# Two query tiles of batch 1 transposed by DMA, and the loads of batch 2 moved behind them

## The chip, the cores and the metric

The kernel runs on one core of a Trainium2 chip. The metric is device time in microseconds: 323.51 us, the median of 3 runs (323.31 to 323.75). One execution was also recorded by the profiler. Its own time is 322.91 us, of which 321.1 us lie between its first and its last instruction. All times below that have a place in the execution count from its first instruction.

## The reference

Eight batches go through cosine-weighted linear attention and then through one gated feed-forward layer. Cut to what matters:

```
r = relu(x); phi(x) = concat(r * cos(theta), r * sin(theta))    # theta = pi/2 * pos / 576
kv  = einsum('bhsf,bhsd->bhfd', phi(k), v)       # per head 128 x 64, sum over 576 positions
z   = sum over positions of phi(k)
x   = (phi(q) @ kv) / (phi(q) @ z + 1e-6)        # 8 batches, 8 heads, 576 positions, 64 wide
xn  = x / sqrt(mean(x*x) + 1e-6) * rms_g         # 4608 rows of 512
out = (silu(xn @ w_gate) * (xn @ w_val)) @ w_out # 512 -> 1536 -> 512
```

q, k and v are 8 x 8 x 576 x 64 in float32, and the weights are 512 x 1536, 512 x 1536 and 1536 x 512.

## The kernel before

**Blocks.** The rows of the feed-forward layer are worked off in nine blocks of 512 rows: block b holds 512 rows of batch b, and one further block ("8") holds the 64 rows that are left over of each batch. A block has 16 steps. In steps 0 to 11 the function `gval_step` computes one slice of 128 hidden columns: four matmuls of the gate into bank `psG`, four of the value into `psV` (line 556), then Silu on ACT and a product on DVE into `hT`. In steps 12 to 15 `out_step` multiplies `hT` by `w_out` (line 574), 12 matmuls for each of four tiles of 128 rows, and ACT copies each result out to `osb`, which SP stores. Block 0 has its own forms of the last steps: `last_step` is its step 11, and `out_first` runs its 48 output matmuls, numbered i = 0 to 47, over four banks.

**Side work.** While the matmuls of block b run, the attention of batch b+1 is made in small pieces, and these pieces are hung by hand on (block, step, place) with `at(...)`. "pe" is ahead of the step's matmuls, "mid" between them, "pre" and "post" ahead of and behind the step's Silu and product. In block 0's last steps `at(0, 12, i, ...)` hangs a piece ahead of output matmul i. For one batch nb the pieces are, in order:

- `load_kv` and `load_q`: 1.1 MB each from DRAM into `raw`, a ring of five buffers. SP issues most of them; for batches 1 and 2 GpSimd (POOL) does.
- `k_phi` (line 294 on DVE, line 292 on ACT) and `v_cast` (line 288): phi(k) and v in bf16.
- `q_phi`, the same for q, in four tiles j of 128 rows, and then the transposition of each tile into `qpT`. From batch 2 on it is a DMA transpose that SP issues (`q_tr_dma`, line 346). In batch 1 all four are made by TensorE (`q_tr_pe`, line 363, eight transposes each) with a copy out of PSUM (`q_tr_evac`).
- `kvz_pe`: the sums kv and z on TensorE (line 394, from batch 3 on line 387), copied to `kvzs` by ACT.
- `nd_pe` (line 449): numerator and denominator of tile j into `psA`; `nd_post`: the division on DVE (lines 489, 492, 499).
- `x_sq`: the mean square on ACT (line 515), and the power -1/2 on POOL (line 520); `x_norm` (line 527) on DVE makes `xn`.
- `x_tr_dma` (line 540): a DMA transpose on SP into `xnT`, which the next block multiplies. Tile 3 of batch 1 is transposed by TensorE instead (`x_tr_pe`, line 546), with a copy by DVE.

Each engine, SP and POOL among them, works off its instructions in the order of the program. So a piece that waits holds up all that stands behind it on its engine. `psG`, `psV` and `psC` have two banks each; `psA` is single, so `nd_pe` of a tile waits for `nd_post` of the tile before.

**Around the change.** In block 0, POOL issues k of batch 2 behind step 8 and v of batch 2 behind step 10. They stand in POOL's DMA queue behind the weights `wo`. `last_step` ends with `nd_pe(1, 0)`, the eight transposes of tile 2, and `nd_post(1, 0)`. In `out_first`, tiles 1 to 3 of batch 1 follow at matmuls 6, 11 and 19, each with the norm and the transpose of the tile before; the transposes of q tile 3 stand at matmul 9, `load_q(2)` and the last norm at 21, and `x_tr` of tile 3 at 43.

Of the kernel before, what the change touches and what calls it, by code (L numbers as in the profile page):

```python
# [10 lines left out]
BF16 = mybir.dt.bfloat16  # L11
# [6 lines left out]
def kernel(  # L18
# [17 lines left out]
    HP = H // 2  # L36
# [10 lines left out]
    V, A, G = nc.vector, nc.scalar, nc.gpsimd  # L47

    ctx.enter_context(tc.manual_schedule())
    one = ctx.enter_context(tc.tile_pool(name="one", bufs=1))  # L50
# [8 lines left out]
    psV = [ps.tile([P, 512], FP32, name=f"psV{i}") for i in range(2)]  # L59
# [10 lines left out]
    def kv_rows(src, b, hps):  # L70
        return src[b, 2 * hps[0] : 2 * hps[1], :, :].rearrange(
            "(hp hh) (s c) d -> (hh s) hp (c d)", hh=2, c=NC
        )

    def wide(b):
        return b > 2
# [21 lines left out]
    def raw_kv(which, b):  # L98
        t = raw_tile(which, b)
        if wide(b):  # L100
            return t[:, :].rearrange("p (h e) -> p h e", h=H)
        return t[:, 0 : HP * NC * D].rearrange("p (hp e) -> p hp e", hp=HP)
# [4 lines left out]
    def load_kv(which, b, hps=(0, HP), eng=nc.sync):  # L107
        src = k if which == "k" else v
        if not wide(b):
            return eng.dma_start(  # L110
                out=raw_kv(which, b)[:, hps[0] : hps[1], :], in_=kv_rows(src, b, hps)
            )
        last = KP if b < B - 1 else KP - 1
        for r0, r1 in ((0, KM), (KM, last)):
            eng.dma_start(
                out=raw_kv(which, b)[r0:r1, :, :], in_=kv_rows5(src, b, r0, r1)
            )
        if last < KP:
            eng.dma_start(
                out=raw_kv(which, b)[last:KP, :, :].rearrange("p h (c d) -> p h c d", d=D),  # L120
                in_=src[b, :, S - 1 : S, :].rearrange("h s d -> s h d").unsqueeze(2)
                .to_broadcast([1, H, NC5, D]),
            )
# [25 lines left out]
    for c0, c1 in ((0, 4), (4, NC)):  # L149
        nc.sync.dma_start(  # L150
            out=raw_kv("k", 0)[:, :, c0 * D : c1 * D],
            in_=kv_rows(k, 0, (0, HP))[:, :, c0 * D : c1 * D],
# [70 lines left out]
    for i in range(3):  # L223
        m, e = math.frexp(left)
# [6 lines left out]
    def g_spread(bank, t):  # L231
# [12 lines left out]
        out=th[:, 0:NTAB], in0=fidx[:, :], scalar1=S - 1.0, scalar2=ang,  # L244
        op0=ALU.min, op1=ALU.mult,
    )
    for c0, c1, i0, less in ((0, 9, 0, 576.0), (13, 14, 13, 64.0), (19, NTAB, 13, 64.0)):
        V.tensor_scalar(
            out=th[64:128, c0:c1], in0=fidx[64:128, i0 : i0 + c1 - c0],
# [4 lines left out]
        out=th[:, NTAB : 2 * NTAB], in0=th[:, 0:NTAB], scalar1=math.pi / 2.0,  # L254
# [4 lines left out]
        out=sel[:, :, :], in_=ident[0:4, 0:4].unsqueeze(2).to_broadcast([4, NDT, P])  # L259
# [57 lines left out]
    def q_phi(eng, b, j, part):  # L317
        o = slice(0, D) if part == 0 else slice(D, F)
        f = cos_of if part == 0 else sin_of
        phi(eng, qp_of((b, j))[:, :, o], raw_q(b)[:, :, j * D : (j + 1) * D], f(9 + j))  # L320
# [23 lines left out]
    def q_tr_dma(b, j):  # L344
        t = qp_of((b, j))
        nc.sync.dma_start_transpose(
            out=qpT[:, :, j * P : (j + 1) * P], in_=t[:, :, :].rearrange("p h f -> p (h f)")
        )
# [10 lines left out]
    def q_tr_pe(b, j, bank):  # L359
        t = qp_of((b, j))  # L360
        dst = bank.bitcast(BF16).rearrange("p (h s) -> p h s", h=H)
        for h in range(H):
            nc.tensor.transpose(dst[:, h, :], t[:, h, :], ident[:, :])  # L363

    def q_tr_evac(eng, b, j, bank):
        dst = bank.bitcast(BF16).rearrange("p (h s) -> p h s", h=H)
        copy(eng, qpT[:, :, j * P : (j + 1) * P], dst)
# [111 lines left out]
    x_of, rs_of, xn_of = {}, {}, {}  # L479
# [31 lines left out]
    def x_sq(b, j):  # L511
        xt = x_of[(b, j)]
        scr = one.tile([P, DM + 1], BF16, name="scr", tag="scr")
        ms = four.tile([P, 1], FP32, name="ms", tag="ms")
        A.activation(  # L515
            out=scr[:, :], in_=xt[:, 0 : DM + 1], func=AF.Square,
            scale=1.0 / math.sqrt(DM), accum_out=ms[:, :],
        )
        rs = four.tile([P, 1], FP32, name="rs", tag="rs")
        G.tensor_tensor(out=rs[:, :], in0=ms[:, :], in1=mhalf[:, :], op=ALU.pow)  # L520
        rs_of[(b, j)] = rs
# [231 lines left out]
    def at(blk, n, where, f, *args):  # L753
        slots.setdefault((blk, n), {}).setdefault(where, []).append((f, args))

    def run(blk, n, where):
        for f, args in slots.get((blk, n), {}).get(where, []):
            f(*args)

    KCS = ((0, 1, 2), (3, 4), (5, 6), (7, 8))  # L760
    KCS5 = ((0, 1), (2,), (3,), (4,))
    for c in range(NC):
        at(0, 5 + c // 3, "post", k_phi, V, 1, c, 0)
        at(0, 5 + c // 3, "post", k_phi, A, 1, c, 1)
    for j in range(4):
        at(0, (8, 8, 9, 10)[j], "post", q_phi, V, 1, j, 0)
        at(0, (8, 9, 10, 10)[j], "post", q_phi, A, 1, j, 1)
        bank = (psC[0], psC[1], psV[0], psV[1])[j]
        if j < 2:
            at(0, 10 + j, "pe", q_tr_pe, 1, j, bank)  # L770
            at(0, 10 + j, "pre", q_tr_evac, V, 1, j, bank)
    at(0, 8, "post", load_kv, "k", 2, (0, HP), G)
    at(0, 9, "post", v_cast, G, 1, (0, 2))
    at(0, 10, "pre", v_cast, V, 1, (2, 4))
    at(0, 10, "post", load_kv, "v", 2, (0, HP), G)

    def q_tr(j, bank):
        q_tr_pe(1, j, bank)  # L780
        q_tr_evac(A, 1, j, bank)

    def x_first(j):
        nd_pe(1, j)
# [11 lines left out]
    def last_step():  # L796
        n = NNT - 1
        g, v = banks_of(0, n)
        run(0, n, "pe")
        half_mm(0, n, wg, g)  # L800
        kvz_pe(1)
        sg = four.tile([P, TB], FP32, name="sg", tag="sg")
        A.activation(out=sg[:, :], in_=g[:, 0:TB], func=AF.Silu)
        kvz_evac(A, 1)
        run(0, n, "pre")
        half_mm(0, n, wv, v)
        nd_pe(1, 0)
        q_tr(2, psV[0])
        nd_post(1, 0)
        V.tensor_tensor(out=hT[:, n, :], in0=v[:, 0:TB], in1=sg[:, :], op=ALU.mult)  # L810
        x_sq(1, 0)
        run(0, n, "post")

    for j, i in ((1, 6), (2, 11), (3, 19)):
        at(0, 12, i, x_first, j)
        at(0, 12, i, x_last, j - 1)
    at(0, 12, 9, q_tr, 3, psV[0])
    at(0, 12, 21, x_norm, 1, 3)
    at(0, 12, 21, load_q, 2)
    at(0, 12, 43, x_tr, 3, psV[0])  # L820
    for nb in range(2, B):
        b = nb - 1
        first = nb == 2
        for i, cs in enumerate(KCS5 if wide(nb) else KCS):
            kb, kn = ((0, 14), (0, 15), (1, 0), (1, 1))[i] if first else (b - 1, 12 + i)
            for c in cs:
                at(kb, kn, "post", k_phi, V, nb, c, 0)
                at(kb, kn, "post", k_phi, A, nb, c, 1)
        for i in range(2):
            vb, vn = ((0, 15), (1, 0))[i] if first else (b - 1, 13 + 2 * i)  # L830
            at(vb, vn, "post", v_cast, V, nb, (2 * i, 2 * i + 2))
        for j in range(4):
            late = j + (nb == 3)
            qb, qn = (b, 1 + j) if first else (b - (late < 2), (14 + late) % 16)
            at(qb, qn, "post", q_phi, V, nb, j, 0)
            at(qb, qn, "post", q_phi, A, nb, j, 1)
            at(qb, qn, "post", q_tr_dma, nb, j)
        kz = 3 if first else 2
        at(b, kz, "pe", kvz_pe, nb)
        at(b, kz, "pre", kvz_evac, A, nb)  # L840
        for j in range(4):
            n = ((6, 8, 9, 11) if first else (4, 6, 8, 10))[j]
            at(b, n, "mid" if n == 9 else "pe", nd_pe, nb, j)
            at(b, n, "pre", nd_post, nb, j)
            at(b, n, "post", x_sq, nb, j)
            m = n + 2 if first and j == 0 else n + 1
            at(b, m, "post", x_norm, nb, j)
            at(b, m, "post", x_tr_dma, nb, j)

    for pair in range(4):  # L850
        b = 2 * pair or 3
        at(*((2, 13), (1, 13), (3, 9), (5, 9))[pair], "post", load_q_tails, pair)
        at(b, 3, "post", q_tails_phi, V, pair, 0)
        at(b, 3, "post", q_tails_phi, A, pair, 1)
        at(b, 3, "post", q_tails_tr_dma, pair)
        at(b, 12, "pe", nd_tails_pe, pair)
        at(b, 12, "pre", nd_post, 2 * pair + 1, 4)
        at(b, 12, "post", x_sq, 2 * pair + 1, 4)
        at(b, 13, "post", x_norm, 2 * pair + 1, 4)
        at(b, 13, "post", x_tr_dma, 2 * pair + 1, 4)  # L860
    for nb in range(3, B):
        b = nb - 2
        for which, n in zip("kvq", {1: (4, 8, 12), 2: (3, 5, 8)}.get(b, (0, 3, 6))):
            if which == "q":
                at(b, n, "post", load_q, nb)
            else:
                at(b, n, "post", load_kv, which, nb)
# [91 lines left out]
```

## Time and profile before

| what | value |
|---|---|
| median of 3 runs | 323.51 us |
| profiled execution, its own time | 322.91 us |
| span of its instructions | 321.1 us |
| TensorE matmul busy | 313.6 us, 98% of the span |
| DVE, ACT, POOL busy | 185.4, 165.8, 40.5 us |
| share of TensorE in the chain that ended last | 94% |
| block 0's output matmuls begin | 42.33 us |
| block 1 begins | 54.09 us |
| block 2 begins | 87.51 us |
| granted TensorE clock | 1.00 |

The busy share says how much of the time an engine worked, not what the end waited for. The chain of work that ended last is followed back from the last instruction to what released each step, and so names what set the end. "q0" is the queue of the DMAs that POOL issues, and "q1" that of SP's; both move their data over the same 16 DMA engines, and a share above 100% means that packets overlap. "To landing" is the time from a DMA's issue until its data is there.

### The profile page before, as it was taken

How to read it: one execution, taken by the hardware profiler on the slowest of the kernel's cores; microseconds unless marked ns; L12 is line 12 of the kernel's file. 1: busy time of each engine (PE TensorE's matmuls, PEld its weight loads, DVE VectorE, ACT ScalarE, POOL GpSimd, SP SyncE). 2: the span in 40 equal slices, each digit the busy share in tenths (PEclk: the TensorE clock that was granted, in tenths of full speed). 3: DMA queues.
4: the chain of work that ended last, by engine and by line, in shares of the span. 5: the costliest groups of instructions: out<-in, count | busy, mean ns of one | idle time of the engine just before them, and what ended most of it. 6: DMA issues, size and time to landing. Idle time of an engine off the chain costs nothing.

```text
span 321.1 us, 6023 instructions
## 1 busy us (share of the span) xinstructions
PE 313.6 (98%) x2274; PEld 162.4 (51%) x2310; DVE 185.4 (58%) x382; ACT 165.8 (52%) x322; POOL 40.5 (13%) x79
## 2 busy tenths in 40 slices
PE   7999999999999999999999999999999999999996
PEld 2689564544454445444544445544544444444444
DVE  7976977668457773777457644781676034204410
ACT  5766756754574466554744575446543233223321
POOL 9771211002001100010001100100011000000000
PEclk9999999999999999999999999999999999999999
DMA  7999999788999999999799959995522500041002
GB/s 232 239 270 269 282 329 227 201 183 190 223 226 211 187 263 187 221 247 182 162 186 230 197 163 200 197 217 163 99 59 41 116 33 0 0 102 31 1 35 98
DMA packets 80092, 53.76 MB, mean 167 GB/s; under 512 B 52235, under 2 KB 74047, under 8 KB 80063
## 3 DMA queue, kind: packets, MB, share of 16 engines
q1 hardware_dynamic: 73110, 41.25, 62.1%
q0 software_dynamic: 6944, 12.13, 15.5%
q8 instruction: 18, 0.29, 0.4%
q14 instruction: 12, 0.09, 0.1%
q10 hardware_dynamic: 8, 0.00, 0.0%
HBM read 37.83 MB, written 9.44 MB: 147 GB/s over the span
## 4 chain that ended last, share of the span: by engine, by line
PE 94%; DMA 2%; DVE 1%; issue 1%; POOL 1%; ACT 0%; POOLq 0%; ACTq 0%
PE psC L574 27%; PE psV L556 27%; PE psG L556 26%; PE psV L643 2%; PE psA L449 2%; DMA vv<-in_v_dram 2%; PE psG L574 2%; PE psG L643 2%; PE psA L387 2%; PE psA L394 1%; PE psA L474 0%; PE psV L363 0%; PE psG L430 0%; PE psC L546 0%; POOL raw L135 0%
## 5 line engine op out<-in xcount | busy, mean ns | idle before, releaser
L571 DVE TENSOR_TENSOR hT<-psV,sg 128x512 bf16<-128x512 f32 x99 | 68.2, 689 | 96.5 <-PE psV L556 64.1
L556 PE MATMUL psV<-xnT,wv 128*128 128x512 bf16 x344 | 89.6, 379 | 0.7 <-issue 0.2
L570 ACT ACTIVATE sg<-psG 128x512 f32<-128x512 f32 x99 | 58.6, 592 | 60.8 <-PE psG L556 52.7
L556 PE MATMUL psG<-xnT,wg 128*128 128x512 bf16 x337 | 88.5, 379 | 0.7 <-issue 0.2
L574 PE MATMUL psC<-wo,hT 128*128 128x512 bf16 (+1 forms) x400 | 88.4, 376 | 0.4
L574 PEld LDWEIGHTS <-hT 128*128 128x128 bf16 x456 | 43.1, 98 | 47.7
L556 PEld LDWEIGHTS <-wv 128*128 128x128 bf16 x400 | 39.0, 98 | 46.8
L556 PEld LDWEIGHTS <-wg 128*128 128x128 bf16 x400 | 37.0, 98 | 39.9 <-DVE xnT L288 0.2
L520 POOL TENSOR_TENSOR rs<-ms,mhalf 128x1 f32<-128x1 f32 x36 | 20.5, 570 | 193.9 <-ACT scr L515 193.7
L286 ACT COPY osb<-psC 128x512 f32<-128x512 f32 x32 | 18.7, 585 | 49.9 <-PE psC L574 46.1
L515 ACT ACTIVATE scr<-xt 128x513 bf16<-128x513 f32 x36 | 22.8, 635 | 23.3 <-DVE xt L499 22.3
L527 DVE SCALAR_TENSOR_TENSOR xn<-xt,rs,gb 128x512 bf16<-128x512 f32 (+1 forms) x37 | 26.9, 730 | 9.9 <-POOL rs L520 9.9
L292 ACT ACTIVATE kp<-raw,tab 128x256 bf16<-128x256 f32 (+2 forms) x51 | 28.8, 607 | 2.4 <-DMA raw<-in_k_dram 2.4
L499 DVE TENSOR_TENSOR xt<-psA,rec 128x512 f32<-128x512 f32 x36 | 24.9, 691 | 1.2
L292 ACT ACTIVATE qp<-raw,tab 128x512 bf16<-128x512 f32 (+1 forms) x36 | 23.3, 666 | 1.2 <-DMA raw<-in_q_dram 1.1
L294 DVE TENSOR_SCALAR kp<-raw,tab 128x256 bf16<-128x256 f32 (+2 forms) x53 | 20.1, 428 | 0.5 <-DMA raw<-in_k_dram 0.5
L294 DVE TENSOR_SCALAR qp<-raw,tab 128x512 bf16<-128x512 f32 (+1 forms) x34 | 15.3, 463 | 4.7 <-DMA raw<-in_q_dram 4.7
L449 PEld LDWEIGHTS <-qpT 128*128 128x128 bf16 x224 | 10.6, 97 | 6.6
L556 PE MATMUL psV<-xnT_tail,wv 128*128 128x512 bf16 x48 | 12.3, 379 | 0.1
L556 PE MATMUL psG<-xnT_tail,wg 128*128 128x512 bf16 x46 | 12.0, 379 | 0.1
L288 DVE CAST vv<-raw 116x1280 bf16<-116x1280 f32 (+1 forms) x13 | 11.1, 857 | 1.3 <-DMA raw<-in_v_dram 1.3
L449 PE MATMUL psA<-kvzs,qpT 128*128 128x65 bf16 x224 | 11.4, 193 | 0.0
(102 smaller groups left out, 177.7 us busy)
## 6 DMA issues: line engine op xcount, KB each, us to landing
out_dram<-osb SPq DMA_DIRECT2D x27, 256.0 KB, 2.3
raw<-in_q_dram SPq DMA_DIRECT2D x6, 1024.0 KB, 9.1
raw<-in_k_dram SPq DMA_DIRECT2D x5, 1120.0 KB, 8.8
raw<-in_v_dram SPq DMA_DIRECT2D x5, 1120.0 KB, 9.4
raw<-in_k_dram POOLq DMA_DIRECT2D x2, 1152.0 KB, 19.2
raw<-in_v_dram POOLq DMA_DIRECT2D x2, 1152.0 KB, 15.7
out_dram<-osb SPq DMA_DIRECT2D x17, 128.0 KB, 2.6
wg<-in_moe_w_gate_dram POOLq DMA_DIRECT2D x3, 512.0 KB, 13.8
```

The source lines that it names most:

```text
L286: A.copy(out=o, in_=i)
L292: A.activation(out=out_ap, in_=in_ap, func=AF.Relu, scale=scale)
L294: eng.tensor_scalar(out=out_ap, in0=in_ap, scalar1=scale, scalar2=0.0, op0=ALU.mult, op1=ALU.max)
L449: nc.tensor.matmul(heads[:, g, hp, :], lhsT=qpT[:, h, j * P : (j + 1) * P], rhs=kvzs[b][:, g, hp * E : (hp + 1) * E], start=True, stop=True,)
L499: V.tensor_tensor(out=xt[:, 0:DM].rearrange("p (hp g d) -> p g hp d", g=2, d=D), in0=heads[:, :, :, 0:D], in1=rec[:, :, :].unsqueeze(3).to ...
L515: A.activation(out=scr[:, :], in_=xt[:, 0 : DM + 1], func=AF.Square, scale=1.0 / math.sqrt(DM), accum_out=ms[:, :],)
L520: G.tensor_tensor(out=rs[:, :], in0=ms[:, :], in1=mhalf[:, :], op=ALU.pow)
L527: V.scalar_tensor_tensor(out=xn_of[(b, j)][:, c], in0=x_of[(b, j)][:, c], scalar=rs_of[(b, j)][:, :], in1=gb[:, c], op0=ALU.mult, op1=ALU. ...
L556: nc.tensor.matmul(bank[:, cols[0] : cols[1]], lhsT=w[:, t, n * P : (n + 1) * P], rhs=x[:, t, cols[0] : cols[1]], start=(t == 0), stop=(t ...
L570: A.activation(out=sg[:, :], in_=g[:, 0:TB], func=AF.Silu)
L571: V.tensor_tensor(out=hT[:, n, :], in0=v[:, 0:TB], in1=sg[:, :], op=ALU.mult)
L574: nc.tensor.matmul(bank[:, 0 : cols[1] - cols[0]], lhsT=hT[:, n, j * P : (j + 1) * P], rhs=wo[:, n, cols[0] : cols[1]], start=(n == 0), st ...
```

## The change

- The transposes of q tiles 2 and 3 of batch 1 are no longer made by TensorE and copied by ACT. A new `q_last` makes their cosine half on DVE at the end of `last_step` (it stood behind steps 9 and 10) and issues a DMA transpose on SP for each.
- POOL issues k of batch 2 at the end of `last_step`, behind the power of tile 0, and v of batch 2 in a new `load_held`, behind a copy of one element that waits for the last norm of batch 1.
- In `out_first` tiles 1, 2 and 3 move to matmuls 8, 16 and 24, the last norm and `load_q(2)` to 25, and `x_tr` to 42.
- The side work of batch 2 moves to later steps of block 1: `k_phi` to steps 0 to 3 (it began in block 0), `v_cast` to steps 2 and 3 and from DVE to POOL, `q_phi` and its transposes from steps 1 to 4 to steps 3 to 6, `kvz_pe` from 3 to 5, `nd_pe` from 6, 8, 9 and 11 to 7, 9, 10 and 12, with each norm one step behind.
- Batch 3: `load_q` moves from step 12 of block 1 to step 14, `k_phi` and `v_cast` one step later, `q_phi` one step later (its first is now behind step 0 of block 2), `nd_pe` in block 2 from steps 4, 6, 8, 10 to 5, 7, 9, 11. The load of the left-over q rows of batches 2 and 3 moves from step 13 of block 1 to step 15.
- The one-row loads for the last row of k and v of batch 7 are issued by POOL and no longer by SP.

```diff
@@ load_kv
         if last < KP:
-            eng.dma_start(
+            G.dma_start(
                 out=raw_kv(which, b)[last:KP, :, :].rearrange("p h (c d) -> p h c d", d=D),
...
-    KCS = ((0, 1, 2), (3, 4), (5, 6), (7, 8))
+    KCS2 = ((0, 1), (2, 3), (4, 5), (6, 7, 8))
...
     for j in range(4):
-        at(0, (8, 8, 9, 10)[j], "post", q_phi, V, 1, j, 0)
+        if j < 2:
+            at(0, 8, "post", q_phi, V, 1, j, 0)
...
-    at(0, 8, "post", load_kv, "k", 2, (0, HP), G)
...
-    at(0, 10, "post", load_kv, "v", 2, (0, HP), G)
-    def q_tr(j, bank):
-        q_tr_pe(1, j, bank)
-        q_tr_evac(A, 1, j, bank)
+    def q_last(j):
+        q_phi(V, 1, j, 0)
+        q_tr_dma(1, j)
+
+    def load_held(b, key):
+        hold = one.tile([1, 1], BF16, name="hold")
+        G.tensor_copy(out=hold[:, :], in_=xn_of[key][0:1, 0:1])
+        load_kv("v", b, eng=G)
@@ last_step
         nd_pe(1, 0)
-        q_tr(2, psV[0])
+        q_last(2)
+        q_last(3)
         nd_post(1, 0)
         V.tensor_tensor(out=hT[:, n, :], in0=v[:, 0:TB], in1=sg[:, :], op=ALU.mult)
         x_sq(1, 0)
+        load_kv("k", 2, eng=G)
...
-    for j, i in ((1, 6), (2, 11), (3, 19)):
+    for j, i in ((1, 8), (2, 16), (3, 24)):
         at(0, 12, i, x_first, j)
         at(0, 12, i, x_last, j - 1)
-    at(0, 12, 9, q_tr, 3, psV[0])
-    at(0, 12, 21, x_norm, 1, 3)
-    at(0, 12, 21, load_q, 2)
-    at(0, 12, 43, x_tr, 3, psV[0])
+    at(0, 12, 25, load_q, 2)
+    at(0, 12, 25, x_norm, 1, 3)
+    at(0, 12, 25, load_held, 2, (1, 3))
+    at(0, 12, 42, x_tr, 3, psV[0])
...
-            kb, kn = ((0, 14), (0, 15), (1, 0), (1, 1))[i] if first else (b - 1, 12 + i)
+            kb, kn = (1, i) if first else (b - 1, 12 + i)
+            if nb == 3:
+                kb, kn = ((1, 13), (1, 14), (1, 15), (2, 0))[i]
...
-            vb, vn = ((0, 15), (1, 0))[i] if first else (b - 1, 13 + 2 * i)
-            at(vb, vn, "post", v_cast, V, nb, (2 * i, 2 * i + 2))
+            vb, vn = (1, 2 + i) if first else (b - 1, 13 + 2 * i)
+            if nb == 3:
+                vn = 14 + i
+            at(vb, vn, "post", v_cast, G if first else V, nb, (2 * i, 2 * i + 2))
...
-            late = j + (nb == 3)
-            qb, qn = (b, 1 + j) if first else (b - (late < 2), (14 + late) % 16)
+            late = j + 2 * (nb == 3)
+            qb, qn = (b, 3 + j) if first else (b - (late < 2), (14 + late) % 16)
...
-        kz = 3 if first else 2
+        kz = 5 if first else 2
...
-            n = ((6, 8, 9, 11) if first else (4, 6, 8, 10))[j]
-            at(b, n, "mid" if n == 9 else "pe", nd_pe, nb, j)
+            n = {2: (7, 9, 10, 12), 3: (5, 7, 9, 11)}.get(nb, (4, 6, 8, 10))[j]
+            at(b, n, "pe", nd_pe, nb, j)
...
-            m = n + 2 if first and j == 0 else n + 1
-            at(b, m, "post", x_norm, nb, j)
-            at(b, m, "post", x_tr_dma, nb, j)
+            at(b, n + 1, "post", x_norm, nb, j)
+            at(b, n + 1, "post", x_tr_dma, nb, j)
...
-        at(*((2, 13), (1, 13), (3, 9), (5, 9))[pair], "post", load_q_tails, pair)
+        at(*((2, 13), (1, 15), (3, 9), (5, 9))[pair], "post", load_q_tails, pair)
...
-        for which, n in zip("kvq", {1: (4, 8, 12), 2: (3, 5, 8)}.get(b, (0, 3, 6))):
+        for which, n in zip("kvq", {1: (4, 8, 14), 2: (3, 5, 8)}.get(b, (0, 3, 6))):
```

## The prediction

> **What bounds the kernel now.** I read the page's busy times first, then the chain of waits between 40 and 60 us, the DMA queues in short windows between 44 and 52 us, and SP's, POOL's, DVE's and ACT's timelines beside them.
>
> ```profile
> PE 313.6 (98%) x2274; PEld 162.4 (51%) x2310; DVE 185.4 (58%) x382; ACT 165.8 (52%) x322; POOL 40.5 (13%) x79
> ...
> 42.04 0.45 PE psV L363 x8
> ...
> 44.68 0.45 PE psV L363 x8
> ...
> 52.95 0.22 PE psV L546 x4
> 53.17 1.08 PE psC L574 x5
> ```
>
> The first line says that TensorE has no reserve. In the chain, every piece from 40 us on is TensorE's and none is a wait, so time is won only by taking work off TensorE, and lost as soon as it waits. The two pieces of line 363 are the transposes that the change removes.
>
> The DMA queues in 46 to 48, 48 to 48.4, 49.4 to 49.6 and 50.6 to 52 us, SP's transposes of `xn` beside them, and the landing of the last one:
>
> ```profile
> q0 software_dynamic: 177, 0.78, 102.7%
> ...
> q0 software_dynamic: 33, 0.15, 100.0%
> ...
> q0 software_dynamic: 7, 0.03, 42.2%
> ...
> q1 hardware_dynamic: 1054, 0.25, 169.5%
> ...
> 45.88 1.29 SPq L540 DMA_TRANSPOSE xnT<-xn  x1
> ...
> 47.65 1.20 SPq L540 DMA_TRANSPOSE xnT<-xn  x1
> ...
> 49.62 1.19 SPq L540 DMA_TRANSPOSE xnT<-xn  x1
> ...
> xnT<-xn SPq DMA_TRANSPOSE x1, 4.3
> ```
>
> Three things are to be seen. First, a transpose issued at 45.88 moved no packet until 48.4, while POOL's queue kept the DMA engines full; it ran engine by engine as they came free of v of batch 2. Second, the transpose issued at 47.65 moved nothing at 49.4 to 49.6, though POOL's queue was down to 42% of the engines; its packets came together with the third one's, after 50.6, when the first was finished everywhere. So transposes go one behind the other. Third, the last, issued at 49.62, landed 4.3 us later, at 53.9, and block 1 begins at 54.09 (its matmuls need all four tiles). This is just in time: there is no reserve behind TensorE.
>
> The last rows are the weights that POOL issued at 23.80, and the two engines that wait for q of batch 3:
>
> ```profile
> wo<-in_moe_w_out_dram POOLq DMA_DIRECT2D x1, 512.0 KB, 21.1
> ...
> 82.33 0.53 SPq L126 DMA_DIRECT2D raw<-in_q_dram  x1
> ...
> 89.65 0.49 DVE L294 TENSOR_SCALAR qp<-raw,tab 128x512 bf16<-128x512 f32 x1 [4.69 <-DMA raw<-in_q_dram]
> ...
> 89.65 0.72 ACT L292 ACTIVATE qp<-raw,tab 128x512 bf16<-128x512 f32 x1 [0.73 <-DMA raw<-in_q_dram]
> ```
>
> The weights land at 44.9, so POOL's queue is busy until then without k and v of batch 2 too. And q of batch 3 already arrives as the last thing at 89.65, 2.1 us after block 2 has begun.
>
> **The change part by part.** The sum is made against the profiled execution, 322.91 us (span 321.1 and 1.8 around it); the median of the runs is 0.60 above it. Ten matmuls of line 574 take 2.16 us, so I count 0.216 each; a step of a block is 8 of them, 1.73 us.
>
> *Transposes off TensorE.* Two pieces of 0.45 us: -0.90. ACT also loses two copies of 1.0 us; it is half idle here, and so this is worth nothing by itself. Block 0's output matmuls then begin at 41.88 and block 1 could begin at 53.2.
>
> *q tile 2 by DMA.* On DVE its cosine half comes behind the copy of tile 1, which ended at 40.8; without the two `q_phi` ahead of that it ends at about 40.1, so SP issues at about 40.6. SP had nothing queued before 45.88. `nd_pe` of tile 2 stands at matmul 16: 41.88 + 16 x 0.216 + 0.24 = 45.58. Bounds: the q transposes of batch 2, with the queues empty, landed in 3.1 us, here 43.7, a wait of 0; counted as 3.1 behind the weights' landing it is 48.0, a wait of 2.4. I take what the first observation gives: engines turn to it as the weights leave them (the small packets thin out between 42.5 and 44.5), 64 packets on each take some 1.6 us (1130 packets in 59.5 to 62.4 were a little over one tile, which took 1.3 to 1.6), and it lands at about 46.5. +0.9 on the path.
>
> *q tile 3 by DMA.* By the second observation it starts when tile 2 is done, 46.3, and lands at 48.4. `nd_pe` of tile 3 at matmul 24 comes at 47.56 + 0.9 = 48.45: 0. Behind this wait on TensorE stand the 24 last output matmuls, and on DVE the norms. The upper bound is the first rival.
>
> *k of batch 2 moved.* ACT is free of the copy that ended at 43.4, so tile 0's power stays near 44.2 and POOL issues k at about 44.7 to 45.4. Nothing of POOL's waits but the later powers (0.55 each, 0.75 for the issue; next power at 46.1). POOL's queue moved 0.81 MB in 44 to 46 us, so k's 1.18 MB take 2.9 us. If it goes behind q tile 3, it has the engines from 48.0 to 51.0. The three `xn` transposes follow, at 0.8 each (1054 packets in 1.4 us are two, and the slowest engine trailed): 53.4, and with the half microsecond from last packet to landing about 54.0 to 54.2. TensorE is there at 53.2 + 0.9 = 54.1. +0.1; bounds 0 (landing 2.6 after the issue, as of an undisturbed `xn` transpose at 73.14) and +1.1 (4.3 after an issue at 50.9). Together block 1 begins at 54.2, against 54.09: **the 0.90 is eaten by the transposes.** Wait and late landing do not add up, since both are the same queue of work.
>
> *Last norm, x_tr, load_q(2).* Tile 3's `xn` ended at 51.18 and comes 0.2 plus 0.9 later, while x_tr stands one matmul earlier, at 51.7 + 0.9: 0.3 us spare, 0. The later `load_q` is issued after the transposes, as before.
>
> *Block 1.* The work of `k_phi` is moved, not changed; DVE is 23.25 of 33.4 us busy there, ACT 19.4, and so it is hidden. k is there by 51, first needed at 56. q and v of batch 2 are both issued near 52.5. Before, q and the stores of block 0 took the queue from 53.1 to 58.9; with 2.9 us more all is in by about 62.7 if nothing goes better. v must land by 60.5 (two POOL casts of 1.15 us, then `kvz_pe` at 54.2 + 5 x 1.73 = 62.85), q by about 62. Zero is taken, since v alone is 2.9 us of this and is not last; the bounds are 0 and +1.5. POOL's casts slow DVE's own (1.42 us beside POOL's, 0.76 alone), which nobody waits for. Tiles at 7, 9, 10 and 12 leave each `nd_post` (1.2 us) a step. The last transpose of batch 2, now behind step 13's store on SP, issues at about 83.8 and lands at 86.4 to 88.1 (2.6 to 4.3) against block 2 at 87.6: 0, bound +0.5.
>
> *q of batch 3.* `load_q` behind the third store of block 1: that store was issued at 85.73, so the load is now at 86.3. q of batch 2 took 6.0 us and q of batch 3 before 7.3 (82.33 to 89.65), with left-over rows beside it that now come later. I take 6.2: 92.5. ACT's first `q_phi` (0.7) stands ahead of Silu of step 1 (0.6), and step 3's gate needs that bank at 87.6 + 1.23 + 3 x 1.73 = 94.0; q may land at 92.6. `nd_pe(3, 0)` at 97.5 needs a transpose that took 4.5 at 90.39: q by 92.2. +0.3; bounds 0 (6.0 and a transpose of 3.1) and +1.4 (7.3).
>
> *The rest.* Two small DMAs of batch 7 go from SP (0.44 to 0.59 each) to POOL, 13% busy: 0. Batch 3's later tiles have their last transpose behind step 12 of block 2, some 7 us ahead of block 3, where 8.4 was the slowest landing: 0, bound +1.
>
> Sum: -0.90 + 0.9 + 0.1 + 0 + 0.3 = +0.4, 323.3 in a profiled execution and **323.9 us** as a median.
>
> **The rivals.** (1) *k overtakes q tile 3.* Tile 3 waits for tile 2 until 46.3, and k, issued at 44.7 to 45.4, may reach idle engines first; loads of SP took 1.4 to 2.2 us from issue to first packet, which is 46.1 to 46.9. If k is first, the queue in front of a transpose is drained first, as at 45.88: k until 49.3, tile 3 until 51.0, landing 51.4. Then 24 matmuls, `nd_pe` and x_tr (5.2 + 0.24 + 0.23) put block 1 at 57.1: +3.0, with q of batch 3 +3.3, **326.8**. It is decided at one point, whether k's first packet is ahead of 46.3.
>
> The Trainium skill, "DMA: Bandwidth & Descriptors", section "Queues, rings and completion order", says that a DMA engine takes turns between the queues that have work, a packet of some 9 to 17 descriptors at a time, up to 64. By that rule k, about one such packet on each engine, would come between tile 3's packets even when it is second, and the rival's 326.8 would hold either way. The trace above speaks against turns (no packet of the transpose in 1.2 us of readiness), so I give the rule no more weight than the race.
>
> (2) *The transposes are served early,* with the weights still queued, and q tile 2 lands by 45.6. Then -0.9 stays, less 0 to 0.3: **322.7**. For it speaks only the 3.1 us of the empty queue.
>
> (3) *q of batch 3 is the wait.* Everything as forecast, but q lands 7.3 us after its issue or later: +1.5, **325.0**.
>
> **How the numbers follow.** Forecast 0.42, with its own range of 323.1 to 324.6 by the bounds of block 1 and q; rival (1) 0.31, (2) 0.16, (3) 0.11. The range of the whole reaches from (2) to (1): 322.7 to 326.8. 0.2% is 0.65 us, about what this kernel's measurement can tell from no change. Faster: (2) and a little, 0.17. Same: 0.33 of the forecast's 0.42. Slower: (1), (3) and the forecast's upper end, 0.50.
>
> **What would show it.** The pieces of line 363 at psV gone, and in their place a wait of TensorE before line 449 at 45 to 47 us for DMA `qpT`; none at 48, or, in rival (1), one of 2 us or more, with q0 full at 46 to 49 and q1 empty. Block 1's start: 54.2, 57.1 or 53.2 in the cases above. Near 92 us a wait of ACT and DVE for `in_q_dram` of more than 3 us, and Silu of step 1 late. The forecast is wrong if transposes are served beside POOL's queue, if block 1 waits for k, q or v, or if DVE's order makes tile 2's issue later than 41.5.

## The result, and the profile after

The changed kernel is slower: 328.31 us, the median of 4 runs (327.33 to 328.91), against 323.50 (323.31 to 323.75) for the kernel before. The ratio is 1.0145, with a 95% interval of 1.0117 to 1.0173. I had forecast 323.9 with a range up to 326.8, so the time lies outside the range. The profiled execution took 327.95 us (span 326.2) and is set against the one of before, 322.91 us (span 321.1); the 5.04 us between them are what has to be found.

Busy times and the chain that ended last, on the page of the changed kernel:

```profile
PE 317.0 (97%) x2294; PEld 161.9 (50%) x2294; DVE 184.4 (57%) x380; ACT 163.6 (50%) x320; POOL 44.5 (14%) x84
...
PE 79%; DMA 9%; DVE 4%; POOL 3%; ACT 2%; issue 1%; SPq 0%; ACTq 0%; POOLq 0%; DVEq 0%
```

TensorE held 94% of the chain before and holds 79% now: DMA, DVE, POOL and ACT have come onto the path. TensorE's waits, by line and by what ended them (us in total, times, longest):

```profile
PE psA L394 <- POOL vv L288: 1.7, 1, 1.7
...
PE psA L474 <- DVE xt L499: 1.0, 1, 1.0
PE psG L430 <- DMA vv<-in_v_dram: 0.8, 1, 0.8
PE psA L449 <- DMA qpT<-qp: 0.6, 1, 0.6
PE psA L449 <- DVE xt L499: 0.6, 1, 0.6
PE psG L556 <- ACT sg L570: 0.2, 1, 0.2
```

Where the blocks begin says what each of them is worth:

| | before | after | longer than before since the line above |
|---|---|---|---|
| `nd_pe(1, 0)` | 41.64 | 42.15 | 0.51 (nothing is changed ahead of it) |
| block 1 | 54.09 | 54.49 | -0.11 |
| block 2 | 87.51 | 91.11 | 3.20 |
| block 3 | 121.29 | 126.38 | 1.49 |
| block 4 | 155.06 | 160.15 | 0 |

The rows of TensorE that begin behind a wait, in the timeline of the changed kernel (start, busy time, what ran, and in brackets the wait and what ended it):

```profile
46.87 0.42 PE L449 MATMUL psA<-kvzs,qpT 128*128 128x65 bf16 x8 [0.61 <-DMA qpT<-qp]
...
64.97 2.04 PE L394 MATMUL psA<-vv,kp 64*128 64x65 bf16 x72 [1.68 <-POOL vv L288]
...
76.81 0.40 PE L449 MATMUL psA<-kvzs,qpT 128*128 128x65 bf16 x8 [0.58 <-DVE xt L499]
...
115.64 0.44 PE L474 MATMUL psA<-kvzs,qpTt 128*64 128x65 bf16 x16 [1.04 <-DVE xt L499]
```

In block 0 q tile 2 costs what the transposes had gained. The two pieces of line 363, the transposes, are gone. In block 1 the sums of batch 2 wait 1.68 us for POOL's first cast of v, and then, in the middle of the 72 matmuls, for the second: from their start to the next matmul it takes 1.97 us here (64.97 to 66.94), and 1.27 where nothing is waited for (61.65 to 62.92, the version with k of batch 3 at step 4, below). That is 2.4 us, and 2.6 is what the block lost besides the 0.58. The 0.58 is a batch 2 tile that finds the single bank `psA` occupied, since its `nd_pe` now stands one step behind the one before. On DVE the product of a step (from 74.37) and a norm (from 74.98) come first, and the division runs only from 75.64 to 76.76. In block 2, 1.04 us are the same kind of wait: the last tile of batch 3 moved to step 11, and the left-over rows follow at step 12. Another 0.31 us of block 2 are the gate of step 3, which needs the bank that Silu of step 1 frees; that Silu stands on ACT behind `q_phi` of batch 3, the row that answers to the one at 89.65 before:

```profile
96.58 0.72 ACT L292 ACTIVATE qp<-raw,tab 128x512 bf16<-128x512 f32 x1 [2.97 <-DMA raw<-in_q_dram]
```

Why the casts were late, in POOL's timeline:

```profile
52.74 0.18 POOL L786 COPY hold<-xn 1x1 bf16<-1x1 bf16 x1 [0.85 <-DVE xn L527]
52.97 0.79 POOL L110 DMA_DIRECT2D raw<-in_v_dram  x1
63.77 2.43 POOL L288 CAST vv<-raw 128x1152 bf16<-128x1152 f32 x2 [10.01 <-DMA raw<-in_v_dram]
```

v was issued at 52.97 and landed 10.6 us later. The DMA queues in 55 to 57, 57 to 58 and 60 to 61 us (packets, MB, share of the 16 engines) say what it waited for; the share of q0, POOL's queue, is v alone here:

```profile
q1 hardware_dynamic: 647, 0.66, 100.8%
...
q1 hardware_dynamic: 278, 0.32, 89.4%
q0 software_dynamic: 17, 0.08, 20.1%
...
q0 software_dynamic: 66, 0.30, 75.1%
...
q1 hardware_dynamic: 70, 0.11, 29.3%
```

What SP had issued, in its timeline:

```profile
52.47 0.45 SPq L126 DMA_DIRECT2D raw<-in_q_dram  x1
53.03 5.82 SPq L592 DMA_DIRECT2D out_dram<-osb  x8
```

SP issued q of batch 2 half a microsecond ahead of v, and the eight stores of block 0 from 53.03 on. The trace tells their packets apart by size: 1 KB for q, 4.6 KB for v, 2 KB for the stores. For 4.6 us after its issue no packet of v moves, while SP's queue has the engines to itself; the first moves at 57.6, when q is almost through (58.0). From then on v shares the engines with the stores, packet for packet: 66 of POOL's queue and 70 of SP's in 60 to 61. So v has to wait for q, but not until SP's queue is empty. Next to k of batch 2, which POOL issued at 45.22 and which had the engines almost to itself, that makes both parts visible: k's first packet moved 1.8 us after the issue and its packets took 4.5 us, v's first moved after 4.6 us and its packets took 5.4. Of the 3.8 us by which v landed later than k (10.6 against 6.8), 2.8 lie behind q and 0.9 in the sharing with the stores.

### The profile page after: what moved, and what is told of

Read it like the earlier page. It is cut to its first block, busy times and chain, and to the rows that moved or that the text cites. A ratio compares the mean times of both kernels' runs of the same rounds, so it can differ in the third digit from the quotient of the medians.

```text
span 326.2 us, 6035 instructions
## 1 busy us (share of the span) xinstructions
PE 317.0 (97%) x2294; PEld 161.9 (50%) x2294; DVE 184.4 (57%) x380; ACT 163.6 (50%) x320; POOL 44.5 (14%) x84
## 4 chain that ended last, share of the span: by engine, by line
PE 79%; DMA 9%; DVE 4%; POOL 3%; ACT 2%; issue 1%; SPq 0%; ACTq 0%; POOLq 0%; DVEq 0%
PE psC L574 25%; PE psG L556 22%; PE psV L556 22%; DMA raw<-in_v_dram 3%; DMA vv<-in_v_dram 2%; PE psV L643 2%; DMA raw<-in_q_dram 2%; PE psG L643 2%; DMA qpT<-qp 2%; PE psA L449 2%; PE psA L387 2%; DVE xn L527 1%; DVE xt L499 1%; ACT sg L570 1%; POOL vv L288 1%
## 5 line engine op out<-in xcount | busy, mean ns | idle before, releaser
L556 PE MATMUL psG<-xnT,wg 128*128 128x512 bf16 x352 | 90.3, 379 | 0.2 <-ACT sg L570 0.2
L570 ACT ACTIVATE sg<-psG 128x512 f32<-128x512 f32 x99 | 58.6, 592 | 57.6 <-PE psG L556 57.5
L288 DVE CAST vv<-raw 116x1280 bf16<-116x1280 f32 (+1 forms) x11 | 9.0, 815 | 0.2 <-DMA raw<-in_v_dram 0.2
```

The lines of the kernel that those rows point to most:

```text
L556: nc.tensor.matmul(bank[:, cols[0] : cols[1]], lhsT=w[:, t, n * P : (n + 1) * P], rhs=x[:, t, cols[0] : cols[1]], start=(t == 0), stop=(t ...
```

## The experiments

The theory (A) after this reading: v stands behind q on the engines, and this and the moved tiles make the loss; put v ahead of q and give `psA` its two steps, and the loss goes. The rivals: (B) the `psA` spacing and POOL's slow casts are the main part; (C) the transposes by DMA cost the time in any order of the loads. Each ratio is against runs of the kernel before on the same chip.

**v ahead of q.** SP issues v ahead of q of batch 2, and nothing is held:

```
+    at(0, 12, 25, load_kv, "v", 2)
     at(0, 12, 25, load_q, 2)
     at(0, 12, 25, x_norm, 1, 3)
-    at(0, 12, 25, load_held, 2, (1, 3))
```

> The changed kernel, but v of batch 2 is issued by SP directly ahead of load_q(2) instead of by POOL behind the held copy; the issue stays near 52.5 us. Theory A (v is late because it stands in POOL's queue and the engines drain SP's queue, q and eight stores, first): v lands some 6 to 7 us after its issue, near 59, the kv matmuls of batch 2 wait for nothing, and the time falls by the 2.6 us of that wait, to 325.7 us. Rival B (v is late because it is issued 14 us later than before, whatever its queue): v lands at 62 or later, and the time stays at 327 to 328.5 us. q of batch 2 then lands near 62.5 in either case, which ACT and DVE would meet at step 3 of block 1.

Measured: 328.86 us, ratio 1.0187 (1.0156 to 1.0219). v landed 5.9 us after its issue, against 10.6, and the wait for it is gone, so the reading of the landing holds. (The run moves v ahead of q and of the stores at once, and from POOL to SP; that q is the larger part comes from the packets above.) The time was not won. TensorE's timeline has a new wait in block 1:

```profile
75.56 0.42 PE L449 MATMUL psA<-kvzs,qpT 128*128 128x65 bf16 x8 [2.04 <-DMA qpT<-qp]
```

SP's timeline says why:

```profile
66.40 1.11 SPq L115 DMA_DIRECT2D raw<-in_k_dram  x2
67.68 6.70 SPq L346 DMA_TRANSPOSE qpT<-qp  x2
```

A transpose of q of batch 2 is issued 1.3 us behind k of batch 3 and takes 7.84 us to land. In the changed kernel, with the sums of batch 2 late, no tile of batch 2 waits for its transpose. One wait stood behind the other, and theory A, which added them up, was wrong on the time.

**Two steps apart.** Batch 2's tiles at steps 6, 8, 10 and 12, and the left-over rows of block 2 one step later, so that on `psA` the two waits above have two steps each:

```
-            n = {2: (7, 9, 10, 12), 3: (5, 7, 9, 11)}.get(nb, (4, 6, 8, 10))[j]
+            n = {2: (6, 8, 10, 12), 3: (5, 7, 9, 11)}.get(nb, (4, 6, 8, 10))[j]
...
-        at(b, 12, "pe", nd_tails_pe, pair)
+        tn = 13 if pair == 1 else 12
+        at(b, tn, "pe", nd_tails_pe, pair)
...
```

> The changed kernel, with two places moved: the tiles of batch 2 at steps 6, 8, 10 and 12 of block 1 (not 7, 9, 10, 12), and the left-over rows of batches 2 and 3 at step 13 of block 2 (not 12, one step behind batch 3's last tile). Theory C (two nd_pe one step apart cost a wait on psA, because DVE's order puts a Silu product and a norm ahead of the division): the waits of 0.6 and 1.2 us vanish, 326.6 us. Rival (the division is late only because the loads made everything late): no more than 0.5 us, 327.8 to 328.3 us.

Measured: 327.4 us, ratio 1.012 (1.0087 to 1.0152). Both waits for `xt` are gone. The median is 0.9 us below the changed kernel's, between the 326.6 of the theory and the 327.8 of its rival, and the intervals of the two ratios overlap, though the waits taken away come to 1.6. The wait for v stays, in TensorE's timeline:

```profile
65.50 2.47 PE L394 MATMUL psA<-vv,kp 64*128 64x65 bf16 x72 [2.17 <-POOL vv L288]
```

What took a part back in the profiled execution (328.06 us, the longest of the four) is in its windows around this wait; the first number behind the five busy times is the granted TensorE clock:

```profile
62.00:64.00 2.00, 1.33 (x7) 0.48 (x5) 1.89 (x6) 2.00 (x5) 0.00 (x0) 1.00 0.59 222
...
66.00:68.00 2.00, 1.96 (x60) 1.83 (x60) 0.00 (x0) 0.00 (x1) 0.73 (x1) 0.52 0.61 121
68.00:70.00 2.00, 1.71 (x6) 0.69 (x7) 0.00 (x0) 0.85 (x2) 0.00 (x0) 0.63 0.88 178
```

Behind the wait TensorE ran at 0.52 and 0.63 of its clock for 4 us: 2 x 0.48 + 2 x 0.37 = 1.7 us lost. So a wait costs more than its own length, in those executions in which the clock falls. This execution also came late to the place of the change: `nd_pe(1, 0)` began at 42.97, 0.82 us behind the changed kernel's, behind code that is the same in both; its trace has the clock at half from 8.05 to 11.47.

**The casts by DVE.** `v_cast` of batch 2 on DVE, as before the change:

```
-            at(vb, vn, "post", v_cast, G if first else V, nb, (2 * i, 2 * i + 2))
+            at(vb, vn, "post", v_cast, V, nb, (2 * i, 2 * i + 2))
```

> The changed kernel, but v of batch 2 is cast by DVE (0.76 us each) and not by POOL (2.4 us for two). If the slow cast is what costs: about 1 us less, 327.3 us. If the load is what costs (theory A or B): DVE now stands itself at step 2 until v lands near 63.6, holds up the products of steps 3 and 4 behind it, and the time is the same or up to 1 us longer, 328 to 329.3 us.

Measured: 329.76 us, ratio 1.0211 (1.0188 to 1.0233). The wait for v is 1.5 us on DVE in place of 1.7 on POOL, but the k features of DVE now come late as well (0.6), and a transpose of q of batch 2 with them (0.79). Block 0's wait for q tile 2 stays as it was (0.64). POOL's slow casts are not the cause, and moving them off DVE did no harm here.

**The transposes alone.** The kernel before, with only q tiles 2 and 3 of batch 1 by DMA and the tiles at the changed kernel's matmuls; k and v of batch 2 are issued early, as before:

```
...
-        q_tr(2, psV[0])
+        q_last(2)
+        q_last(3)
...
-    for j, i in ((1, 6), (2, 11), (3, 19)):
+    for j, i in ((1, 8), (2, 16), (3, 24)):
...
```

> The kernel before, with one part of the change alone: q tiles 2 and 3 of batch 1 by DMA transpose, and the tiles at matmuls 8, 16, 24, 25 and 42; k and v of batch 2 are loaded early as before, all later steps as before. Theory D (a DMA engine empties the queue that it works on before it turns to another): the first transpose gets no packet until v of batch 2 is through near 48.5 to 50, nd_pe of tile 2 waits until about 50.5, and block 1 begins 4 to 5 us later: 327 to 329 us. The rule of turns between queues: it is served between the packets of the loads and lands by 44 to 47, and the time is 322.7 to 324.5 us.

Measured: 332.27 us, ratio 1.0277 (1.0246 to 1.0308), the slowest of all. TensorE's timeline:

```profile
53.40 0.62 PE L449 MATMUL psA<-kvzs,qpT 128*128 128x65 bf16 x8 [7.30 <-DMA qpT<-qp]
53.83 2.75 PE L574 MATMUL psC<-wo,hT 128*128 128x512 bf16 x6
```

The DMA queues in 46 to 48 us:

```profile
q0 software_dynamic: 157, 0.68, 92.0%
q1 hardware_dynamic: 158, 0.04, 9.2%
```

The transpose of q tile 2, issued at 40.63, landed 12.7 us later, so theory D was on the right side, with 327 to 329 us, which is too low. But the engines did not first empty POOL's queue. For 4.0 us the transpose moved no packet, while the weights and the first of k went through. From 44.6 on the two queues moved packet for packet, as the lines show for 46 to 48: 157 and 158. In such turns a transpose gets little, since its packets are small (256 bytes, by the trace, against 4.6 KB of k and v): 0.04 MB beside 0.68. The 1024 packets of a q tile were therefore not through before k and v were. So the loads of batch 2 had to go back if these transposes were to go to the DMA, and the two parts of the change can't be judged apart.

The Trainium skill ("DMA: Bandwidth & Descriptors", section "Queues, rings and completion order") says that an engine takes turns between the queues that have work, packet by packet. The equal counts here agree with that, and so do those of v and the stores above (whether the page's packet is the profile's, no run shows). The silence ahead of them (4.0 us here, 4.6 for v) does not show such turns, and what ends it no run here shows. The landing by 44 to 47 that I had worked out from turns didn't come true either: it left out the silence, and how little a turn is worth to a small packet.

The matmuls behind the wait take 0.46 us (2.75 for 6) where 0.216 is usual, at a granted clock of 0.50.

**k of batch 3 behind q's transposes.** On top of v ahead of q, k of batch 3 is issued behind step 6 of block 1:

```
-        for which, n in zip("kvq", {1: (4, 8, 14), 2: (3, 5, 8)}.get(b, (0, 3, 6))):
+        for which, n in zip("kvq", {1: (6, 8, 14), 2: (3, 5, 8)}.get(b, (0, 3, 6))):
```

> As e1 (v of batch 2 issued by SP ahead of q), and k of batch 3 is loaded behind step 6 of block 1, behind the four q transposes of batch 2, and no longer behind step 4, between them. Theory E (in e1 v was early enough, but the wait of 2.0 us for a q transpose that queues behind k of batch 3 took the place of the wait for v): that wait is gone, and the profile shows block 1 in some 33.5 to 34.5 us instead of 35.4; 326 to 327 us. Rival (q of batch 2 itself is too late, whatever stands between): the wait moves to the first q tile and the time stays at 328 to 329 us.

Measured: 325.93 us, ratio 1.0082 (1.006 to 1.0103). The wait of 2.04 is gone, and this time the gain is there: 2.9 us less than with v ahead of q alone. What is left is mostly the two waits for `xt`, 0.6 and 1.0.

**All the waits named so far.** As the last, with batch 2's tiles at 7, 9, 11 and in the middle of 12, the left-over rows at 13, and q of batch 3 one step earlier:

```
-            n = {2: (7, 9, 10, 12), 3: (5, 7, 9, 11)}.get(nb, (4, 6, 8, 10))[j]
+            n = {2: (7, 9, 11, 12), 3: (5, 7, 9, 11)}.get(nb, (4, 6, 8, 10))[j]
-            at(b, n, "pe", nd_pe, nb, j)
+            at(b, n, "mid" if first and j == 3 else "pe", nd_pe, nb, j)
...
-        for which, n in zip("kvq", {1: (6, 8, 14), 2: (3, 5, 8)}.get(b, (0, 3, 6))):
+        for which, n in zip("kvq", {1: (6, 8, 13), 2: (3, 5, 8)}.get(b, (0, 3, 6))):
```

> As e5, and the two places with tiles one step apart are stretched (batch 2's tiles at 7, 9, 11 and in the middle of step 12; the left-over rows at step 13 of block 2), and q of batch 3 is loaded one step earlier, behind step 13. If the waits found so far are all that the change costs, and the DMA transposes of the q tiles are a wash in block 0 (0.1 us less in the profile), the time comes back to the kernel before: 323.0 to 324.2 us. If there is a further cause (a slower clock behind the waits excepted, which goes with them), it stays above 325 us.

Measured: 325.57 us, ratio 1.0068 (1.0047 to 1.0088). The waits for `xt` are gone, and one of 2.8 us for the transposes of `xn` stands at the start of block 2. The 323.0 to 324.2 us of the theory did not come.

**Later tiles.** As the last, with tiles 2 and 3 of batch 1 at matmuls 20 and 27, the loads and the last norm at 28, and `x_tr` at 45:

```
-    for j, i in ((1, 8), (2, 16), (3, 24)):
+    for j, i in ((1, 8), (2, 20), (3, 27)):
...
```

> As e6, with q tiles 2 and 3 needed later in block 0: at output matmuls 20 and 27 (not 16 and 24), norm and loads at 28, x_tr at 45. If the 0.9 us of TensorE work that the change removes is lost only in the wait for q tile 2 (0.75 us in the profile): that wait is gone, block 1 begins 0.6 to 0.8 us earlier than in e6, and the time is 322.4 to 323.4 us, at or under the kernel before. If the DMA transposes of xn then land last: no more than 0.2 us less than e6, and a wait of block 1's first matmul for xnT.

Measured: 326.0 us, ratio 1.0085 (1.0057 to 1.0113). The wait for q tile 2 is gone, and from `nd_pe(1, 0)` to block 1 it takes 53.04 - 41.32 = 11.72 us, against 12.45 before. Of the 0.90 that the transposes free, 0.73 is won when nobody waits for them. It is not seen in the time, because of 2.4 us at block 2's start:

```profile
89.20 1.02 PE L556 MATMUL psG<-xnT,wg 128*128 128x512 bf16 x4 [2.44 <-DMA xnT<-xn]
```

**Transposes by TensorE again.** As "all the waits", with q tiles 2 and 3 transposed by TensorE at the places of before, so that only the moved loads and side work are left:

```
...
-        q_last(2)
-        q_last(3)
+        q_tr(2, psV[0])
...
-    for j, i in ((1, 8), (2, 16), (3, 24)):
+    for j, i in ((1, 6), (2, 11), (3, 19)):
...
+    at(0, 12, 9, q_tr, 3, psV[0])
...
```

> As e6, but q tiles 2 and 3 are transposed by TensorE again, at the places that they had in the kernel before (tiles at matmuls 6, 11, 19; norm and loads at 21; x_tr at 43); only the loads and later steps are the change's. If the DMA transposes are a wash: the same as e6 within 0.4 us, with 0.9 us more of TensorE work and no wait for q tile 2. If they are a gain by themselves: 0.5 to 0.9 us longer than e6; if they are a loss, that much shorter, because loads are issued earlier without the wait.

Measured: 325.04 us, ratio 1.0056 (1.0036 to 1.0076), with a wait of 1.56 us at block 2's start, for which the profile shows no releaser. It lies 0.5 us under "all the waits", and the two intervals overlap. In that placement the transposes by DMA are a wash. So taking them back does not take the loss away: 1.9 us of it are left, of which 1.56 are that wait. The two kernels below, with these transposes by DMA and without the loss, put theory C out as the main cause.

**q of batch 3 back at step 14.** As "later tiles", with q of batch 3 at step 14 as in the changed kernel, and k of batch 3 at step 5 in one kernel and at step 4 in the other:

```
-        for which, n in zip("kvq", {1: (6, 8, 13), 2: (3, 5, 8)}.get(b, (0, 3, 6))):
+        for which, n in zip("kvq", {1: (5, 8, 14), 2: (3, 5, 8)}.get(b, (0, 3, 6))):
```

> As e7 (all waits stretched, q tiles needed later), with k of batch 3 behind step 5 of block 1 (not 6) and q of batch 3 behind step 14 (not 13). Theory F (what is left in e7, a wait of 2.4 us of block 2 for xnT, comes from SP's queue: k of batch 3 one load later makes v of batch 3 later, and the last two xn transposes stand behind v, and q next to them): the wait falls to 0 to 0.8 us, q of batch 3 costs 0.3 to 0.6 us in its place, 323.4 to 324.6 us. Rival (the wait comes from tile 3's own place in the middle of step 12): the wait stays near 2.4 us, 325.5 to 326.5 us.

> As e9, with k of batch 3 behind step 4, as in the changed kernel; tile 2 of batch 2 is needed at step 11 here, 1.7 us later than in e1. Theory F: no wait of block 2 for xnT, a wait of 0 to 1 us for the q transpose behind k of batch 3, 323.2 to 324.6 us. Rival as in e9: a wait near 2.4 us for xnT, 325.5 us or more.

Measured over 10 runs each, with 19 of the kernel before: 323.57 us, ratio 1.0017 (1.0003 to 1.0032), and 323.61 us, ratio 1.0007 (0.9993 to 1.0021). The loss is gone (with k at step 5 up to 0.3% may be left); a gain is not there. k at step 4 and q at step 14 are the changed kernel's own places, so what takes the loss away is v ahead of q, the two steps between the tiles and the later q tiles of batch 1, together; how much each of them is worth by itself no run shows. All of TensorE's waits in the profiled execution with k at step 5, of which the last ends before 13 us:

```profile
PE psC L598 <- DVE warm L164: 1.2, 1, 1.2
PE psG L430 <- DMA vv<-in_v_dram: 0.5, 1, 0.5
```

This execution took 322.45 us, 0.46 less than the profiled one of before. The wait at block 2's start was there in the three kernels with q of batch 3 at step 13 (1.6 to 2.8 us), and never above 0.2 in the kernels with v ahead of q and q of batch 3 at step 14. But q is not what takes the engines from the last transpose. With "later tiles" q is issued at 83.98, its first packet moves at 88.06, and the last packet of the transposes ends at 88.2. What differs is v of batch 3, ahead of the transposes in SP's queue, as the first half of theory F had it. SP begins to issue it at 73.28 with "later tiles" and at 74.23 with k at step 4, but its last packet ends at 83.46 in the one and at 81.37 in the other: with k at step 6, k's own packets run until 77.3, and with k at step 4 they are through at 72.4. That is 2.1 of the 3.2 us by which the last transpose is through later (88.2 against 85.1); the other 1.1 stay open. In the kernel with k at step 6 and q at step 14 v ends late too (83.7); there TensorE reached block 2 only at 88.42, and with "later tiles" at 86.76 (89.20 - 2.44), so nothing was left to wait for.

**The last kernel once more.** The same kernel with k at step 4, in another execution and on another chip:

> The kernel of e10 once more, one look. In e10's profiled execution TensorE waited for nothing behind 13 us, and its time, 322.61 us, is 1.0 us under the median of e10's own ten times. If those other times carry waits of the same sort, this execution shows 0.3 to 1.5 us of TensorE waits for qpT, xnT or q of batch 3 between 45 and 100 us and takes 323.2 to 324.4 us; if they carry only a later start (the first loads), the time differs before 13 us and nowhere else.

Measured: 323.56 us, span 321.8, against 322.61 and 320.8 in the first profiled execution. TensorE's timeline now has two waits in blocks 1 and 2 that the first did not show:

```profile
74.62 0.42 PE L449 MATMUL psA<-kvzs,qpT 128*128 128x65 bf16 x8 [0.58 <-DMA qpT<-qp]
...
94.00 1.02 PE L556 MATMUL psG<-xnT,wg 128*128 128x512 bf16 x3 [0.22 <-ACT sg L570]
```

The transposes behind k of batch 3 and the q of batch 3 are just in time in one execution and just late in the next. That is how a version without a wait in its best execution can come to the same median as before: the reserve behind TensorE is nil at these two places. These are two executions; what the other nine waited for was not recorded.

**v not held.** The changed kernel, with v issued by POOL directly behind k and no copy that holds it:

```
         load_kv("k", 2, eng=G)
+        load_kv("v", 2, eng=G)
...
-    at(0, 12, 25, load_held, 2, (1, 3))
```

> The changed kernel, but POOL issues v of batch 2 directly behind k at the end of block 0's last_step, with no hold. If a DMA engine empties POOL's queue before it serves SP's transposes: v lands near 54 and the kv matmuls wait for nothing, but the three xn transposes of block 0 start only near 52.5 to 54 and block 1 begins 1 to 2.5 us later than in the changed kernel; the time is 326 to 328 us, so that the hold moves the wait and does not make it. If transposes are served beside the loads: block 1 begins as before, near 54, and the time is 325 to 326 us.

Measured: 331.25 us, ratio 1.025 (1.0209 to 1.0291). This is above the 326 to 328 us of the theory. v lands ahead of its use, and other transfers are waited for in its place:

```profile
PE psA L449 <- DMA qpT<-qp: 2.9, 2, 2.2
PE psG L556 <- DMA xnT<-xn: 2.2, 1, 2.2
```

The 2.2 us for `xnT` are the start of block 1, at 56.46 and 2.0 us behind the changed kernel's, as forecast: the transposes of `xn` run behind k and in turns with v (100 packets of each queue in 51.5 to 53 us). Of the 2.9 us for `qpT`, 0.66 are block 0's wait for q tile 2, and 2.19 the wait of "v ahead of q" again, for a transpose of q of batch 2 issued 1.4 us behind k of batch 3. The hold does not make the loss; without it the same 1.2 MB are in the way of something that is needed sooner.

## Why the prediction was wrong

*Block 0 came out as forecast.* I had -0.90 for the transposes and +0.9 for q tile 2: TensorE came to `nd_pe` of tile 2 0.78 us late (46.87 - 44.36 - 8 x 0.216), the transpose landed at 46.8 (forecast 46.5), tile 3 was not waited for, and k did not overtake it (k's first packet moved at 47.0, the last of SP's queue at 47.2). That is 1.8 us behind k's issue; the rival had counted with 1.4 to 2.2 from SP's loads, which by their packets in the trace of before took 1.2 to 1.8. The sum from `nd_pe(1, 0)` to block 1 is -0.11, forecast +0.1. The first rival didn't happen: the measured time is nearer to its 326.8 than to mine, but for another reason, and not in block 0. With k too late to meet tile 3, block 0 says nothing on turns between the queues.

*q of batch 3 was sized right.* Forecast +0.3 by a landing 6.2 us after the issue; it took 6.7, ACT waited for it, and with Silu of step 1 late behind it the gate of step 3 began 0.31 late.

*The step that failed is block 1.* I wrote "Zero is taken, since v alone is 2.9 us of this and is not last", with +1.5 as its upper bound. v came late. It landed at 63.6, 3.1 us behind the 60.5 that I had worked out as its due time, and the term measured 2.6 us. What decides it I had read myself from the trace of before: a transfer that comes to busy engines moves nothing until the one in front is nearly through (no packet from 45.88 to 48.4). I used that for transposes of SP behind loads of POOL, and not for POOL's v behind SP's q, issued at nearly the same time, where it cost 2.8 us, with 0.9 more for the stores. v ahead of q shows it: 5.9 us and no wait. Had I put v last, my own "all in by 62.7" would have been its landing, and 62.7 + 2.4 of casts against 62.85 gives +2.3. That this is close to what was measured would have been luck in part: 58.9 and 2.9 make 61.8, the prediction doesn't say where the other 0.9 comes from, and v was not last behind the stores but shared the engines with them. The stronger form, that a queue is emptied before the other is served, is wrong: in the changed kernel, with the transposes alone and with v not held the two queues go on packet for packet once both have begun. The prediction spoke against turns from the trace of before, and that trace shows only the silence.

*Two waits were not in the sum.* I wrote of batch 2's tiles that they "leave each `nd_post` (1.2 us) a step". A step is not enough where `nd_post` stands on DVE behind the product of the step and a norm (74.37 to 75.64 for the two): +0.58. And of batch 3's tiles, now one step later, I checked the last transpose against block 3 but not the left-over rows behind it on `psA`: +1.04. Two steps apart shows both.

*The clock was not in it either.* Runs of the changed kernel in which the granted clock was 1.000 took 327.33 and 327.95 us, those with 0.995 on average 328.67 and 328.91. All runs of the kernel before had at least 0.999.

Together: 0.51 ahead of anything that was changed, -0.11, 3.20 (2.6 for v, 0.58 for the bank), and 1.49 (0.31 for q, 1.04 for the left-over rows, some 0.1 not assigned) make 5.09 us, where the spans differ by 5.1.

## What to carry to other kernels

When a load moves, write down for each queue what is on the same DMA engines when it is issued, and work out its landing by that. In these traces what had begun went through first, and then two queues shared packet for packet, so that small packets got little beside large ones; a rule read at one pair of queues is to be tried on every pair that meets. In a stretch in which the engines are booked throughout, moving one load moves the wait to the next transfer, and waits that stand behind each other are seen one at a time, so a gain is to be claimed only when the whole row of them has been followed to the end. And of a stage that is moved a step, look at what shares its buffers on either side, the left-over work too.

## What the runs showed that I had not expected

- *The clock falls after a wait of about 2 us.* It did so behind waits of 2.17 us (to 0.52) and 2.2 us (to 0.50 in 58 to 60 us, with v not held), and with the transposes alone it was still 0.50 four us behind the end of the 7.3. With the casts by DVE two waits of 1.47 and 0.58 us close together were enough. It does not always: behind one of 2.04 us, with v ahead of q, it stayed at 1.00 in the profiled execution (326.92 us), while the other three runs of that kernel had 0.995 on average and took 328.1 to 330.2. Behind the 2.80 us of "all the waits" it also stayed at 1.00, and behind the 2.44 us of "later tiles" it fell to 0.57 and 0.58 in the next 4 us, so the length alone does not decide. The runs of "later tiles" show the two cases side by side: 325.17 and 325.37 us at 1.000, 326.64 and 326.72 at 0.995.
- The Trainium skill, "TensorE: Matmul & The Clock Gate", section "Part 1: The HAM clock gate (the "warmup" mystery)", says that the array drops to half its clock after an idle window of some 3.4 us, by a window that runs freely, and comes back after as long a busy one. The half clock agrees with the 0.50 measured here, and the play from run to run agrees with the free window. The time at half the clock agrees too: 3.4 us in the trace of "two steps apart" (66.08 to 69.49) and in that of "later tiles" (90.28 to 93.69). The waits that were enough here were shorter, 2.2 to 2.4 us.
- *The same code at either end varies by half a microsecond and more.* `nd_pe(1, 0)` began between 41.3 and 42.97 us in the profiled executions, and from the last 24 matmuls to the end of the span it took 4.3 us before the change (321.1 - 316.82) and 4.8 with k of batch 3 at step 5 (320.7 - 315.90). A gain of 0.9 us up to the last matmuls came out as 0.4 in that span.
